# Sketched attention and squared-ReLU feed-forward on one core: another prologue, with S first, k features in column tiles, w_in in two loads and four pieces of v through GpSimd's queue

## The chip, the core and the metric

The kernel runs on one core of a Trainium2 chip. The metric is the device time of one execution in microseconds (us); lower is better. Several executions were timed, and one more was taken by the hardware profiler. All durations below come from that profiled execution.

## What is computed

Polynomial-sketch attention without a softmax, then a feed-forward block. For each of 4 batches and 4 heads (sequence 1088, head size 32):

```python
a, b = S1 @ x, S2 @ x                 # 8 values each, for x = q and x = k
phi(x) = outer(a, b)                  # 64 features per position
kv = sum_s phi(k_s) v_s^T             # 64 x 32
z  = sum_s phi(k_s)                   # 64
attn = phi(q) kv / (phi(q) z + 1e-6)
x = attn, heads side by side          # 4352 tokens x 128
out = relu(x @ w_in)**2 @ w_out       # w_in 128 x 2048, w_out 2048 x 128
```

All in float32; the product with w_in uses the rounded type fp32r, so w_in has to be converted ("cast") on the chip once.

## The kernel before, in words

The feed-forward part is TensorE's work: tokens are cut into ten chunks of columns (256, 384, 448, 448, 512 ...). For each chunk there are 16 blocks of w_in. A *unit* is one or two blocks: a first product `pg` (L589), a relu on ScalarE (`gt`, L598), a square on ScalarE or VectorE (`g`, L606 or L608), and a second product `po` (L627) that sums over the 16 blocks.

The attention part makes the columns of `xT` that these chunks read. Batches 1 to 3 are prepared while earlier chunks run. Batch 0 can't be: its first 256 columns are made in a **prologue**, written out by hand, in which nothing of the feed-forward runs. From there on a small planner in the kernel (`_Order`) places all remaining tasks on the engines, by due times and by cost estimates in its code; the engines then run in that fixed order. The rest of batch 0 (12 blocks of 32 columns from block 8, then 16 from block 20) is planned work too.

The prologue, in the order in which it feeds itself:

- Loads. SP issues k of batch 0 in two column halves, q's first 256 columns, then v, further q, w_in in four loads and w_out in four. ScalarE issues S1 and S2 (L217, L218) into `s_nat` and two pieces of v. A load that reuses one of the eight semaphores for hardware loads waits until the load eight before it has landed, so SP's list also waits in places. v of batch 0 comes as two times four pieces: first the row blocks t = 0 to 3 of four groups of partitions, then t = 4 to 8 of the same groups ("the later pieces").
- S is turned around by VectorE (`s_T`, L688), and thirteen small copies on GpSimd, VectorE and ScalarE spread it into block-diagonal tables: `sf` (for k, L693; a plain copy, L708) and `sq` (for q, L696 to L703).
- TensorE meanwhile runs ten matmuls of ones (`warm`, L678) that compute nothing.
- VectorE transposes k into `kt0` (L291) in three parts and q's first 256 columns into `qT` (L297).
- TensorE: `kf` (L314), nine fp32 products of 128 x 128 k columns with `sf`; then `x` (L729), q's sketch with `sq`, in two halves q0(0) and q0(1). ScalarE copies half of each result (`kb`, `qb`), and VectorE multiplies (`kp`, L330, four instructions; `qp`, L748).
- TensorE: `kvp` (L390), 36 products of `kp` with v, t by t; the first 16 need the first pieces of v, the rest the later ones.
- The closing chain: `bd` (L764) spreads `kvp`; the denominator `den` (L794) goes through a transpose, a reciprocal and another transpose (`dT`, `rd`, `bc`); the numerator times `bc` is `xT` (L819), which the first `pg` reads. Beside it: `zm`, the sketch with z (L801, copied to `sw` by L806), the spread of kv (`a_rep`, L433, copied by L439), and the sketch `qc` of the next 12 blocks (L304), whose two transposes of q were made by VectorE ahead of `bd`.

GpSimd converts the four quarters of w_in (L671), two in the prologue and two as planned work.

The piece of code that sets the two parts of v:

```python
def first(b, t, p):
    return NT * p + t if b else 4 * p + t if t < 4 else 16 + 5 * p + t - 4
def load_v(eng, b, p, t0=0, t1=NT):
    n = 32 * ((t1 if p < 3 else min(t1, NT - 2)) - t0)
    eng.dma_start(
        _ap(vn[b % 2], 32 * p, 32, 32 * t0, [[32 * NT, H], [1, n]]),
        bass.AP(v.tensor, v.offset + b * H * S * D + 32 * first(b, t0, p),
                [[G * D, 32], [S * D, H], [1, n]]),
    )
```

Of the kernel before, what the change touches and what calls it, by code (L numbers as in the profile page):

```python
# [104 lines left out]
def kernel(  # L105
# [20 lines left out]
    LU = 4  # L126
    W0, W3, W4 = 10, 1, 1
    ND, QT, WI, KL, QL = 2, 3.0, (1.0, 1.9), (30.0, 12.0), 4.0
# [27 lines left out]
    def sb(name, cols, dt=F32, rows=128):  # L156
        return cpool.tile([rows, cols], dt, tag=name, name=name)
# [9 lines left out]
    w_in32, w_o, w_in = sb("w_in32", 2048), sb("w_o", 2048), sb("w_in", 2048, F32R)  # L167
    s_nat, s_T = sb("s_nat", 32, rows=32), sb("s_T", 32, rows=32)

# [11 lines left out]
    def load_q(eng, b, c0, c1):  # L181
        eng.dma_start(
            qn[b % 2][:, c0:c1],
            bass.AP(q.tensor, q.offset + b * H * S * D + c0, [[G * D, 128], [1, c1 - c0]]),
        )
# [10 lines left out]
            bass.AP(  # L196
                v.tensor, v.offset + b * H * S * D + 32 * first(b, t0, p),
                [[G * D, 32], [S * D, H], [1, n]],
            ),
        )  # L200

    def load_wi(eng, c):
        eng.dma_start(
            w_in32[:, 512 * c : 512 * c + 512], moe_w_in[:, 512 * c : 512 * c + 512]
        )
# [9 lines left out]

    nc.vector.memset(s_nat[:], 0.0)
    nc.scalar.dma_start(s_nat[0:8, :], S1[:, :])  # L217
    nc.scalar.dma_start(s_nat[8:16, :], S2[:, :])  # L218
    load_k(nc.sync, 0, 0, 512)
# [8 lines left out]
    load_v(nc.scalar, 0, 3, 0, 4)  # L228
    for p in range(4):
        load_v(nc.sync, 0, p, 4, NT)  # L230
    load_q(nc.sync, 0, 256, 640)
    load_wi(nc.sync, 0)
    load_wi(nc.sync, 1)
    load_q(nc.sync, 0, 640, S)
    load_wo(nc.sync, 0)
    load_wi(nc.sync, 2)
    load_wi(nc.sync, 3)
    load_wo(nc.sync, 1)
# [5 lines left out]

    sf, sq = sb("sf", 96), sb("sq", 256)
    nc.vector.memset(sf[:, 0:64], 0.0)
    nc.gpsimd.memset(sq[:], 0.0)
    nc.gpsimd.memset(_ap(vn[0], 96, 32, 32 * (NT - 2), [[32 * NT, H], [1, 64]]), 0.0)
# [62 lines left out]
    def a_kf(t0, n, pool, tag):  # L311
        kf = pool.tile([128, 512], F32, tag=tag, name="kf")
        for t in range(n):
            nc.tensor.matmul(  # L314
                _ap(kf, 0, 128, 32 * t, [[32 * n, 2], [1, 32]]),
                kt0[:, 128 * (t0 + t) : 128 * (t0 + t) + 128],
                sf[:, 0:64],
            )
# [370 lines left out]
    for h, eng in (
        (0, nc.gpsimd.tensor_copy), (1, nc.vector.tensor_copy), (2, nc.scalar.copy),  # L690
        (3, nc.vector.tensor_copy),
    ):
        eng(  # L693
            _ap(sf, 32 * h, 32, 8 * h, [[32, 2], [1, 8]]), _ap(s_T, 0, 32, 0, [[8, 2], [1, 8]])
        )
    nc.gpsimd.tensor_copy(  # L696
        _ap(sq, 0, 32, 0, [[8, 8], [1, 8]]), _ap(s_T, 0, 32, 8, [[0, 8], [1, 8]])
    )
    nc.scalar.copy(
        _ap(sq, 0, 32, 128, [[8, 8], [1, 8]]), _ap(s_T, 0, 32, 0, [[1, 8], [0, 8]])  # L700
    )
    for h, eng in ((1, nc.scalar.copy), (2, nc.gpsimd.tensor_copy), (3, nc.scalar.copy)):
        eng(  # L703
            _ap(sq, 32 * h, 32, 64 * (h % 2), [[128, 2], [1, 64]]),
            _ap(sq, 0, 32, 0, [[128, 2], [1, 64]]),
        )
    for h in range(H):
        nc.gpsimd.tensor_copy(sf[32 * h : 32 * h + 32, 64:96], s_T[:, :])  # L708
    for h in range(H):
# [43 lines left out]
    for y in range(2):  # L753
# [27 lines left out]
    a_bd(0)  # L781

    nc.gpsimd.tensor_copy(zero_a[:, 0:1], st[0, "kp"][:, 256 * NT - 1 : 256 * NT])
    for c in range(2):
        cast_wi(c)
    nc.gpsimd.memset(sfk[:], 0.0)
    for h in range(H):
        o = 16 * (h % 2)
        nc.gpsimd.tensor_copy(sfk[32 * h : 32 * h + 32, o : o + 16], s_T[:, 0:16])
    num0 = psf.tile([128, 512], F32, tag="pg", name="num0")  # L790
# [21 lines left out]
    keep_warm(W4)
    dT0 = wpool.tile([128, 256], F32, tag="dT0", bufs=1, name="dT0")
# [30 lines left out]

    for c in (2, 3):
        O.add(("wi", c), {"POOL": 0.7}, 0.5 * c, [], on(cast_wi, c), at=WI[c - 2])
    prev = {"qc": None}
    PEL, M, T0 = 0.3, 5.0, 1.5

    def q_tasks(b, i0, nb, key):  # L850
# [3 lines left out]
        names = []  # L854
        if (b, i0) != (0, AC[0][1][0]):
            for x in range(2):
                i1, n1 = i0 + x * (nb // 2), nb // 2
                n1 = min(n1, G - i1)
                names.append(("qT", b, i1))
                O.add(  # L860
                    names[-1], {"DVE": dve(32 * n1)}, k0 - 1.5,
                    ([("qn", b)] if b else []) + prev["qTuse"], on(a_qT, b, i1, n1),
                    at=QT if i0 == 20 else 0.0,
                )
# [139 lines left out]
    for u in range(NU):  # L1004
# [90 lines left out]
```

## Time and profile before

| | |
|---|---|
| time, median of 3 runs | 187.05 us (186.77 to 187.11) |
| time of the profiled execution | 186.58 us |
| its span, first to last instruction | 184.8 us |
| TensorE matmul busy | 180.0 us, 97% |
| ScalarE, VectorE, GpSimd busy | 135.0, 120.0, 36.8 us |
| first product of the feed-forward (`pg`) | at 13.54 us |
| loads, share of the 16 DMA engines busy, 0 to 4.6 us | 0.57 (179 GB/s) |
| the same, 4.6 to 8.2 us | 0.75 (214 GB/s) |
| the same, 10.54 to 13.54 us | 0.98 (300 GB/s) |

The profile lists busy time by engine, groups of instructions by source line, the chain of work that ended last, and a timeline. "PE" is TensorE's matmul side, "PEld" its weight loads, "DVE" VectorE, "ACT" ScalarE, "POOL" GpSimd, "SP" the engine that only issues loads and stores; a "q" behind a name is that engine's instruction queue, where a load is issued. A row of the timeline gives start, duration, engine, line, what is written from what, a count if rows are merged, and in brackets how long the engine stood idle before it and what ended that.

### The profile page before, as it was taken

Reading aid. Unit: us, or ns where it says so; the run is one execution under the profiler, and the core shown is the slowest. Engines: PE = TensorE matmul, PEld = TensorE weight load, DVE = VectorE, ACT = ScalarE, POOL = GpSimd, SP = SyncE. Lnnn points to the kernel's source line nnn. Section 1 sums busy time; section 2 is a strip of 40 time slices with the busy share of each in tenths; the row PEclk is TensorE's granted clock in tenths of the full one; section 3 lists DMA queues with packets and bytes.
Section 4 is the critical chain, followed back from the end, with each engine's and each line's share of the span. In section 5 each row is a group of like instructions: output and inputs, shape, how many; then the busy total and the mean of one; then the engine's idle time right before and its main releaser. Section 6 shows DMA issues by size and latency. Waiting matters only on the chain.

```text
span 184.8 us, 3784 instructions
## 1 busy us (share of the span) xinstructions
PE 180.0 (97%) x1418; PEld 104.9 (57%) x1418; DVE 120.0 (65%) x259; ACT 135.0 (73%) x264; POOL 36.8 (20%) x162
## 2 busy tenths in 40 slices
PE   8998999999999999999999999999999999999992
PEld 2867766656555466555554545545555545555791
DVE  4979879959983598699436984998243334222430
ACT  3409869759968787699577975794777777777760
POOL 3745407138300000870000004820000000000000
PEclk9999999999999999999999999999999999999999
DMA  5799800100039700000871200003003000300211
GB/s 179 205 278 322 200 8 2 28 4 0 0 46 239 173 0 4 4 0 14 200 199 20 41 0 5 0 0 49 11 0 59 0 0 5 52 0 0 33 28 28
DMA packets 24673, 11.25 MB, mean 61 GB/s; under 512 B 18000, under 2 KB 23120, under 8 KB 24656
## 3 DMA queue, kind: packets, MB, share of 16 engines
q1 hardware_dynamic: 24144, 10.82, 24.8%
q10 hardware_dynamic: 512, 0.20, 0.4%
q8 instruction: 11, 0.18, 0.4%
q14 instruction: 6, 0.05, 0.1%
HBM read 8.78 MB, written 2.23 MB: 60 GB/s over the span
## 4 chain that ended last, share of the span: by engine, by line
PE 97%; ACT 0%; DVE 0%; issue 0%
PE po L627 60%; PE pg L589 18%; PE nd L542 4%; PE warm L678 3%; PE kvp L408 2%; PE pol L622 2%; PE po L622 2%; PE qc L304 2%; PE kvp L390 1%; PE kf L314 1%; PE kc L344 1%; PE x L729 1%; ACT gt L598 0%; PE den L794 0%; PE num L794 0%; PE den L754 0%
## 5 line engine op out<-in xcount | busy, mean ns | idle before, releaser
L627 PE MATMUL po<-g,w_o 128*128 128x512 f32 (+3 forms) x288 | 123.5, 547 | 0.0
L598 ACT ACTIVATE gt<-pg 128x512 f32<-128x512 f32 (+3 forms) x145 | 75.1, 568 | 34.6 <-PE pg L589 34.2
L627 PEld LDWEIGHTS po<-g,w_o 128*128 128x128 f32 x288 | 53.1, 188 | 31.8 <-issue 23.6
L589 PE MATMUL pg<-xT,w_in 128*128 128x512 f32 (+3 forms) x160 | 68.9, 513 | 0.5 <-ACT gt L598 0.5
L606 ACT ACTIVATE g<-gt 128x512 f32<-128x512 f32 (+2 forms) x105 | 59.9, 602 | 1.4
L608 DVE TENSOR_TENSOR g<-gt 128x512 f32<-128x512 f32 (+3 forms) x40 | 26.6, 666 | 40.6 <-ACT gt L598 40.0
L589 PEld LDWEIGHTS pg<-xT,w_in 128*128 128x128 f32 x160 | 28.9, 190 | 29.1 <-ACT gt L598 10.6
L449 POOL COPY kv<-kvt 32x64 f32<-32x64 f32 x48 | 12.3, 256 | 64.8 <-DVE kvt L426 62.7
L503 POOL COPY rd<-rc 32x9 f32<-32x9 f32 (+2 forms) x80 | 16.5, 206 | 11.2 <-DVE rc L495 7.8
L512 DVE STREAM_SHUFFLE qa<-qc 128x576 f32<-128x576 f32 (+2 forms) x20 | 11.6, 652 | 0.0
L527 DVE TENSOR_TENSOR qp<-qa,qb 128x576 f32<-128x576 f32 (+2 forms) x20 | 10.8, 606 | 0.0
L361 DVE TENSOR_TENSOR kp<-fs 128x576 f32<-128x576 f32 x12 | 8.4, 752 | 0.1
L475 DVE STREAM_TRANSPOSE qt<-qc 128x576 f32<-128x576 f32 (+2 forms) x10 | 5.8, 615 | 3.7 <-PE qc L304 3.7
L631 DVE STREAM_TRANSPOSE oT<-po 128x512 f32<-128x512 f32 (+3 forms) x9 | 5.9, 652 | 2.4 <-PE po L627 2.4
L542 PE MATMUL nd<-qp,kv 32*32 32x288 f32 (+2 forms) x320 | 6.8, 353 | 0.0
L559 DVE TENSOR_TENSOR xT<-nd,bc 128x576 fp32r<-128x576 f32 (+2 forms) x10 | 5.6, 600 | 1.2 <-PE nd L542 1.2
L552 DVE STREAM_TRANSPOSE bc<-rd 128x576 f32<-128x576 f32 (+2 forms) x10 | 5.8, 605 | 0.7 <-POOL rd L503 0.6
L542 PEld LDWEIGHTS nd<-qp,kv 32*32 32x32 f32 x320 | 3.8, 103 | 3.9 <-issue 2.9
L512 DVE STREAM_SHUFFLE qb<-qc 128x576 f32<-128x576 f32 (+2 forms) x10 | 6.0, 649 | 0.0
L297 DVE STREAM_TRANSPOSE qT<-qn 128x192 f32<-128x192 f32 (+3 forms) x11 | 5.9, 566 | 0.0
L678 PE MATMUL warm<-const-bfloat16-1.0 128*128 128x512 bf16 x12 | 5.0, 571 | 0.8 <-PEq L1079 0.8
L622 PE MATMUL pol<-w_o,g 128*128 128x128 f32 x32 | 5.7, 275 | 0.0
(96 smaller groups left out, 92.6 us busy)
## 6 DMA issues: line engine op xcount, KB each, us to landing
kn<-in_k_dram SPq DMA_DIRECT2D x3, 544.0 KB, 4.9
qn<-in_q_dram SPq DMA_DIRECT2D x3, 544.0 KB, 6.9
vn<-in_v_dram SPq DMA_DIRECT2D x9, 144.0 KB, 5.3
w_in<-in_moe_w_in_dram SPq DMA_DIRECT2D x4, 256.0 KB, 5.0
w_o<-in_moe_w_out_dram SPq DMA_DIRECT2D x4, 256.0 KB, 7.9
out_dram<-oT SPq DMA_DIRECT2D x12, 64.0 KB, 2.0
out_dram<-oT SPq DMA_DIRECT2D x8, 56.0 KB, 2.3
out_dram<-oT SPq DMA_DIRECT2D x8, 48.0 KB, 2.2
```

The lines of the kernel that those rows point to most:

```text
L449: nc.gpsimd.tensor_copy(_ap(st[b, "kv"], 32 * c, 32, 64 * h, [[32, E], [1, 32]]), _ap(st["kvt"], 32 * h, 32, 0, [[64, E], [1, 32]]),)
L503: nc.gpsimd.tensor_copy(st[b, "rd", i0][32 * h : 32 * h + 32, n * c : n * c + n], st["rc"][32 * c : 32 * c + 32, n * h : n * h + n],)
L512: nc.vector.stream_shuffle(in_=banks(st[b, "qc", i0], 2 * x, 0, m), out=_ap(st[b, which, i0], 0, 128, 2 * m * x, [[m, 2], [1, m]]), mask=m ...
L527: nc.vector.tensor_tensor(out=st[b, "qp", i0, e][:, r], in0=st[b, f"qa{e}", i0][:, r], in1=st[b, "qb", i0][:, r], op=mult,)
L542: nc.tensor.matmul(nd[32 * h : 32 * h + 32, 512 * c : 512 * c + m], kv[r, o : o + 32], qp[r, m * h : m * h + m], start=(e == 0), stop=(e = ...
L589: nc.tensor.matmul(st["pg", u][:, n * i : n * i + n], w_in[:, 128 * (d0 + i) : 128 * (d0 + i) + 128], xT[:, c0 : c0 + n],)
L598: nc.scalar.activation(gt[:, 0:w], st["pg", u][:, 0:w], Relu)
L606: nc.scalar.activation(g2[:, 0:w], gt[:, 0:w], Square)
L608: nc.vector.tensor_tensor(out=g2[:, 0:w], in0=gt[:, 0:w], in1=gt[:, 0:w], op=mult)
L622: nc.tensor.matmul(po[x // 128][:, 0:128], g[:, x : x + 128], w, start=(d == 0), stop=(d == NB - 1),)
L627: nc.tensor.matmul(po[0][:, 0:n], w, g, start=(d == 0), stop=(d == NB - 1))
L678: nc.tensor.matmul(t_[:, 0:cols], nc.const_aps.tensor(1.0, (128, 128), mybir.dt.bfloat16), nc.const_aps.tensor(1.0, (128, cols), mybir.dt. ...
```

## The change

Only the prologue is rewritten, with what follows from it in the planner's list.

- **S.** S1 is issued by ScalarE without waiting for a memset, S2 by SP as its first load. The thirteen copies go. A selection table `sel` is made on GpSimd by two copies from the identity matrix; four fp32 matmuls of `s_nat` with `sel` (K = 16, 32 x 80 each) make all tables for k and the plain S in PSUM; ScalarE copies them once into `ss`. `s2f` is then transposed at once by VectorE, ahead of k's transposes. `sq` is made by two products on GpSimd (128 x 128 each, two inputs).
- **Dummy matmuls:** five, then the four of S, then three; later one rather than two.
- **k features:** each of the nine 128-column products is cut into four of 32 columns, whose outputs lie in four groups of 32 partitions.
- **Loads:** w_in comes in two loads of 1024 columns rather than four of 512, the first one ahead of q's second part; one w_out load moves ahead of q's third part. The four later pieces of v leave SP and are issued by GpSimd, after the two copies into `sel` and ahead of `sq`.
- **Casts of w_in:** two quarters on ScalarE behind `qb`, two on GpSimd behind its small work; none is planned work any more.
- **The end of the prologue:** the copy of `kvt` goes from VectorE to ScalarE; the numerator is placed ahead of the spread of kv; the two transposes for `qc` and `qc` itself leave the prologue and become planned work.

The core of the diff:

```diff
-    W0, W3, W4 = 10, 1, 1
+    W0, W1, W3 = 5, 3, 1
...
-    nc.vector.memset(s_nat[:], 0.0)
     nc.scalar.dma_start(s_nat[0:8, :], S1[:, :])
-    nc.scalar.dma_start(s_nat[8:16, :], S2[:, :])
+    nc.sync.dma_start(s_nat[8:16, :], S2[:, :])
     load_k(nc.sync, 0, 0, 512)
     load_k(nc.sync, 0, 512, S)
     load_q(nc.sync, 0, 0, 256)
...
-    for p in range(4):
-        load_v(nc.sync, 0, p, 4, NT)
+    load_wi(nc.sync, 0)
     load_q(nc.sync, 0, 256, 640)
-    load_wi(nc.sync, 0)
     load_wi(nc.sync, 1)
+    load_wo(nc.sync, 0)
     load_q(nc.sync, 0, 640, S)
-    load_wo(nc.sync, 0)
-    load_wi(nc.sync, 2)
-    load_wi(nc.sync, 3)
...
-    nc.gpsimd.memset(sq[:], 0.0)
+    sq, sel = sb("sq", 256), sb("sel", 320, rows=16)
+    nc.vector.memset(sel[:, :], 0.0)
...
+    nc.gpsimd.tensor_copy(
+        _ap(sel, 0, 16, 0, [[88, 4], [32, 2], [1, 8]]), _ap(iden, 0, 16, 0, [[0, 4], [8, 2], [1, 8]])
+    )
+    nc.gpsimd.tensor_copy(
+        _ap(sel, 0, 16, 64, [[80, 4], [1, 16]]), _ap(iden, 0, 16, 0, [[0, 4], [1, 16]])
+    )
+    for p in range(4):
+        load_v(nc.gpsimd, 0, p, 4, NT)
...
-            nc.tensor.matmul(
-                _ap(kf, 0, 128, 32 * t, [[32 * n, 2], [1, 32]]),
-                kt0[:, 128 * (t0 + t) : 128 * (t0 + t) + 128],
-                sf[:, 0:64],
-            )
+            for c in range(4):
+                o = 128 * (t0 + t) + 32 * c
+                nc.tensor.matmul(
+                    _ap(kf, 32 * c, 32, 32 * t, [[32 * n, 2], [1, 32]]),
+                    kt0[:, o : o + 32],
+                    sf,
+                )
...
-        nc.gpsimd.tensor_copy(
+        (nc.scalar.copy if c < 2 else nc.gpsimd.tensor_copy)(
             w_in[:, 512 * c : 512 * c + 512], w_in32[:, 512 * c : 512 * c + 512]
         )
...
+    sp = psf.tile([128, 512], F32, tag="po", name="sp")
+    for h in range(H):
+        nc.tensor.matmul(
+            sp[32 * h : 32 * h + 32, 0:80], s_nat[:, :], sel[:, 80 * h : 80 * h + 80]
+        )
+    nc.scalar.copy(ss[:, :], sp[:, 0:80])
+    nc.vector.transpose(s2f[:, :], _ap(ss, 0, 128, 72, [[0, 4], [1, 8]]))
+    keep_warm(W1)
     a_kT0(0, 4)
-    nc.vector.transpose(s_T[:, :], s_nat[:, :])
...
+    for x in range(2):
+        nc.gpsimd.tensor_tensor(
+            out=_ap(sq, 0, 128, 128 * x, [[64, 2], [8, 8], [1, 8]]),
+            in0=_ap(ss, 0, 128, 72 - 8 * x, [[0, 2]] + [[[0, 8], [1, 8]], [[1, 8], [0, 8]]][x]),
+            in1=_ap(own_q, 0, 128, 0, [[1, 2], [0, 8], [0, 8]]),
+            op=mult,
+        )
...
-    for i0 in (8, 14):
-        a_qT(0, i0, 6)
...
+    for c in range(4):
+        cast_wi(c)
     a_bd(1)
...
+    nc.scalar.copy(st["kvt"][:, :], st[0, "kvp"][:, 0:128])
...
+    nc.scalar.copy(sw[0][:, 16:24], x0[:, 384:392])
+    nd0(num0, 0)
     a_rep(x0, 256)
-    nc.scalar.copy(sw[0][:, 16:24], x0[:, 384:392])
     a_rep_kv(x0, 256)
-    nd0(num0, 0)
     st["warm"] = psf.tile([128, 512], F32, tag="po", name="warm")
     keep_warm(W3)
-    a_qc(0, *AC[0][1])
-    keep_warm(W4)
```

More of the change, by code (lines that the diff above doesn't have):

```diff
@@ L167 @@
     w_in32, w_o, w_in = sb("w_in32", 2048), sb("w_o", 2048), sb("w_in", 2048, F32R)
-    s_nat, s_T = sb("s_nat", 32, rows=32), sb("s_T", 32, rows=32)
+    s_nat, ss, s2f = sb("s_nat", 32, rows=16), sb("ss", 80), sb("s2f", 32)
+    sf, s_T = ss[:, 0:64], ss[:, 64:80]
     sw = [sb(f"sw{i}", 32) for i in range(2)]
@@ L203, in load_wi @@
         eng.dma_start(
-            w_in32[:, 512 * c : 512 * c + 512], moe_w_in[:, 512 * c : 512 * c + 512]
+            w_in32[:, 1024 * c : 1024 * c + 1024], moe_w_in[:, 1024 * c : 1024 * c + 1024]
         )
@@ L240 @@
     load_wo(nc.sync, 3)
-    sf, sq = sb("sf", 96), sb("sq", 256)
-    nc.vector.memset(sf[:, 0:64], 0.0)
-    nc.gpsimd.memset(sq[:], 0.0)
+    sq, sel = sb("sq", 256), sb("sel", 320, rows=16)
+    nc.vector.memset(sel[:, :], 0.0)
     nc.gpsimd.memset(_ap(vn[0], 96, 32, 32 * (NT - 2), [[32 * NT, H], [1, 64]]), 0.0)
@@ L262 @@
     make_identity(nc, iden[:])
-    own_f, s2f, zm = sb("own_f", 16), sb("s2f", 32), sb("zm", 32)
+    own_f, zm = sb("own_f", 16), sb("zm", 32)
+    own_h, own_q = sb("own_h", 4), sb("own_q", 2)
+    nc.gpsimd.tensor_copy(
[6 more added lines that the diff above has]
+        load_v(nc.gpsimd, 0, p, 4, NT)
+    nc.vector.tensor_reduce(
+        out=own_h[:, :], in_=_ap(iden, 0, 128, 0, [[32, 4], [1, 32]]), op=add, axis=AX
+    )
+    nc.vector.tensor_tensor(out=own_q[:, :], in0=own_h[:, 0:2], in1=own_h[:, 2:4], op=add)
     nc.vector.tensor_reduce(
@@ L267 @@
     )
-    nc.vector.memset(kT[:, S:SP], 0.0)
-    nc.vector.memset(qT[:, S:SP], 0.0)
     mask_a = [[4 * e + l // 8 for l in range(32)] for e in range(E)]
@@ L463, in a_w @@
             in0=_ap(st[b, "kvp"], 0, 128, 32, [[64, E], [8, 4], [1, 8]]),
-            in1=_ap(sf, 0, 128, 72, [[0, E], [0, 4], [1, 8]]),
+            in1=_ap(ss, 0, 128, 72, [[0, E], [0, 4], [1, 8]]),
             op=mult,
@@ L686 @@
     keep_warm(W0)
-    a_kT0(0, 4)
-    nc.vector.transpose(s_T[:, :], s_nat[:, :])
[L689 to L694, printed above, removed]
-        )
[L696 to L708, printed above, removed]
+    sp = psf.tile([128, 512], F32, tag="po", name="sp")
[6 more added lines that the diff above has]
+    keep_warm(W1)
+    a_kT0(0, 4)
+    for x in range(2):
[4 more added lines that the diff above has]
+            op=mult,
+        )
     for h in range(H):
@@ L715 @@
     for w in sw:
-        nc.gpsimd.tensor_copy(w[:, :], sf[:, 64:96])
+        nc.gpsimd.memset(w[:, 16:32], 0.0)
+        nc.gpsimd.tensor_copy(w[:, 0:16], s_T)
+    nc.gpsimd.tensor_tensor(
+        out=_ap(sfk, 0, 128, 0, [[16, 2], [1, 16]]),
+        in0=_ap(ss, 0, 128, 64, [[0, 2], [1, 16]]),
+        in1=_ap(own_q, 0, 128, 0, [[1, 2], [0, 16]]),
+        op=mult,
+    )
+    nc.gpsimd.memset(kT[:, S:SP], 0.0)
+    nc.gpsimd.memset(qT[:, S:SP], 0.0)
     nc.gpsimd.memset(_ap(pd, 0, 128, 8, [[9, 4 * NT], [1, 1]]), 1e-6)
@@ L745 @@
             a_kv0(t)
-    nc.vector.transpose(s2f[:, :], _ap(sf, 0, 128, 72, [[0, 4], [1, 8]]))
     nc.vector.tensor_tensor(
@@ L769, in a_bd @@
         )
+    for c in range(4):
+        cast_wi(c)
     a_bd(1)
-    st["kvt"] = wpool.tile([128, 128], F32, tag="kvt", name="kvt")
-    nc.vector.tensor_copy(st["kvt"][:, :], st[0, "kvp"][:, 0:128])
     nc.vector.tensor_tensor(
@@ L781 @@
     a_bd(0)
[L783 to L789, printed above, removed]
+    st["kvt"] = wpool.tile([128, 128], F32, tag="kvt", name="kvt")
+    nc.scalar.copy(st["kvt"][:, :], st[0, "kvp"][:, 0:128])
     num0 = psf.tile([128, 512], F32, tag="pg", name="num0")
@@ L843, in on @@
         return lambda eng: f(*args)
-    for c in (2, 3):
-        O.add(("wi", c), {"POOL": 0.7}, 0.5 * c, [], on(cast_wi, c), at=WI[c - 2])
     prev = {"qc": None}
@@ L854, in q_tasks @@
         names = []
[L855 to L864, printed above, removed]
+        for x in range(2):
+            i1, n1 = i0 + x * (nb // 2), nb // 2
+            n1 = min(n1, G - i1)
+            names.append(("qT", b, i1))
             O.add(
-                ("qc", b, i0), {"PE": 0.75}, k0 - 1.0, names + [("w", b)], on(a_qc, b, i0, nb),
-                rings=[("att", 1)], lag=PEL,
-            )
-        else:
-            O.add(("qc", b, i0), {"PE": 0.01}, -99.0, [], lambda eng: None, rings=[("att", 1)])
+                names[-1], {"DVE": dve(32 * n1)}, k0 - 1.5,
+                ([("qn", b)] if b else []) + prev["qTuse"], on(a_qT, b, i1, n1),
+                at=QT if i0 == 20 else 0.0,
+            )
+        O.add(
+            ("qc", b, i0), {"PE": 0.75}, k0 - 1.0, names + [("w", b)], on(a_qc, b, i0, nb),
+            rings=[("att", 1)], lag=PEL,
+        )
         prev["qTuse"] = [("qc", b, i0)] if i0 + nb == 4 * NT else []
@@ L888, in q_tasks @@
                 ("rl", b, i0, c), {"POOL": 0.8}, k0 + 0.1 * c, [], on(a_rl, b, i0, nb, c),
-                uses=[("rc", b, i0)] + [("wi", 3)], rings=[("rd", 2)] if c == 0 else [],
+                uses=[("rc", b, i0)], rings=[("rd", 2)] if c == 0 else [],
             )
@@ L1016 @@
                 mm1s[i], {"PE": n / 2400 + 0.01},
-                tu[u] - LA + 0.001 * i, xt + [("wi", (d0 + i) // 4)] * (u < NB), on(ffn1, u, i),
+                tu[u] - LA + 0.001 * i, xt, on(ffn1, u, i),
                 rings=[("pg" if u else "po", 2)] if i == 0 else [], lag=0.05,
```

## The prediction

> **What bounds the kernel now.** I read the chain of waits first, by line, then the timeline of the first 25 us, where alone the change acts.
>
> ```profile
> PE 180.0 (97%) x1418; PEld 104.9 (57%) x1418; DVE 120.0 (65%) x259; ACT 135.0 (73%) x264; POOL 36.8 (20%) x162
> ...
> PE 97%; ACT 0%; DVE 0%; issue 0%
> ```
>
> The chain is TensorE almost throughout, so behind the first `pg` only TensorE work counts, and the change leaves that work as it is: in the built programs the later order is the same but for a few swaps. What can move is the start of the first `pg`, 13.54. It hangs on the prologue, some of whose matmuls are dummies. The timeline's rows of 0 to 24 us (start, duration, engine, line, tiles):
>
> ```profile
> 1.80 0.29 POOL masks.py:199 TENSOR_SCALAR_AFFINE_SELECT iden<-iden 128x128 f32<-128x128 f32 x1
> ...
> 3.37 0.71 DVE L291 STREAM_TRANSPOSE kt<-kn 128x512 f32<-128x512 f32 x1 [0.82 <-DMA kn<-in_k_dram]
> ...
> 4.95 2.08 PEld L314 LDWEIGHTS kf<-sf,kt 128*128 128x128 f32 x18 [0.66 <-POOL sq L696]
> ...
> 4.98 2.19 PE L314 MATMUL kf<-sf,kt 128*128 128x64 f32 x18
> ...
> 5.63 0.40 DVE L297 STREAM_TRANSPOSE qT<-qn 128x256 f32<-128x256 f32 x1
> ...
> 5.96 2.71 DVE L330 TENSOR_TENSOR kp<-kf,kb 128x512 f32<-128x512 f32 x4
> ...
> 7.11 1.14 PE L729 MATMUL x<-qT,sq 64*128 64x256 f32 x8
> ...
> 8.17 2.32 PE L390 MATMUL kvp<-vn,kp 128*64 128x64 f32 x72
> ...
> 10.54 0.29 DVE L764 TENSOR_TENSOR bd<-kvp,own_p 128x128 f32<-128x128 f32 x1 [0.39 <-PE kvp L390]
> ```
>
> Read it backwards. `bd` at 10.54 waits for `kvp`, and from `bd` to the first `pg` is a fixed 3.00 us (den, dT, rd, bc, xT). `kvp` runs without a gap from 8.17, 2.37 before `bd`. Its first factor was ready at about 6.6 (5.96 plus the first of four products), so it waited only for TensorE: `x` came first (1.06 from 7.11 to 8.17), and `x` stood behind `kf`, which ended at 7.17. So the prologue is bound by TensorE from 4.98, by VectorE's `kp` just behind (ended 8.67), and by loads ahead of that.
>
> **Part by part.**
>
> *S and `kf`.* Gone: thirteen copies, whose last one released `kf` at 4.95. New: four S matmuls, a ScalarE copy, `s2f`. S is issued at about 0.73 instead of 0.92 and 1.52; k's two loads and q's first one move back by one issue, 0.3 to 0.4 (S1's issue took 0.58, S2's 0.29). Five dummies at 0.42 end at 2.9, S matmuls about 3.3, the copy of 80 columns (rows of `kb`: 0.21) 3.6, `s2f` (0.19) 3.8. k's first half lands at 3.7 (was 0.73 + 2.6 = 3.35), its transpose (0.71) ends at 4.5. So `kf` may begin 0.45 earlier. Column tiles replace 18 weight loads at 0.116 (2.08/18) by 72 of a quarter of the columns. The nearest row, `kvp`'s half-width tiles, takes 2.32/72 = 0.032 each, 2.3 in all, no gain; if four run beside each other as `kvp`'s two do, half of it, 1.1. I take 1.1; at 2.3 `kf` would end near 7.1 as now.
>
> *VectorE's order* then sets the pace. k's second half landed at 1.19 + 3.0 = 4.2 and q at 1.66 + 3.7 = 5.4. Now they come 0.35 later at issue, and ScalarE's two pieces of v (64 KB each, at 1.90 and 3.37 so far) go out ahead of 2 us beside them: 128 KB at 300 GB/s is 0.4. I take k at 5.0 and q at 5.5 to 5.8, from no change to 0.8 later. Two transposes (0.84) and `qT` (0.40) end at 6.25, `kp` begins 6.2 rather than 5.96. After `qT`, `x` may start at 6.4, and 1.06 + 2.37 later `bd` at **9.85**: 0.69 earlier. That is the floor if nothing else is late.
>
> *GpSimd's queue* is what can be late. Four loads are put between the copies into `sel` and the products `sq`, and all of `x`, hence `kvp`, stands behind `sq` on TensorE. From 1.10 (the memset of v's padding) to the end of the identity at 2.09 are 0.99; without the memset of `sq` ahead they start at 0.73, so 1.72, and two copies (0.19 to 0.23 each) make 2.15. An issue costs I. Two products of 128 columns: the nearest one-input rows are 0.29; with two inputs I take 0.40 each (0.3 to 0.6), 0.8. `sq` is done at 2.95 + 4I. TensorE starts the second half of `x` 0.16 later (as `den` behind `bd`), it takes 0.53, then 2.37: `bd` at **6.01 + 4I**. What else stands behind the four issues has time: `irep` (1.32 for four copies), a memset (0.31) and `sw` (0.35) end near 9.4, and are read by the spread of kv and by `qc`, at 11.5 and later. SP in turn has four v issues and two of w_in fewer, so q's later parts, w_out and batch 1 go out earlier; none of them was waited for by TensorE, so I count nothing.
>
> No load was issued by GpSimd in this trace, so I is bounded by the rows of v's pieces on the other queues:
>
> ```profile
> L194 SPq DMA_DIRECT2D vn<-in_v_dram x10: 311/431/1802, 2.1 to 16.1; - x10
> L194 ACTq DMA_DIRECT2D vn<-in_v_dram x2: 343/360/378, 1.9 to 3.4; - x2
> ```
>
> The columns are shortest, median and longest issue in ns. Below is 0.31, the shortest (four cost 1.2, the floor holds); above 1.80, the longest, in which SP was held up. No row is nearer to an issue whose descriptors a processor writes, so I take the middle, 1.05: `bd` at 10.21, 0.33 earlier. Each 0.1 of I is 0.4 us; the prologue breaks even at 1.13.
>
> On this the Trainium skill speaks against the change: "DMA: Bandwidth & Descriptors", section "Latency and other measured facts", puts the first byte of a load of GpSimd's queue at about 1 us, made by its cores, against about 0.6 for the hardware queues. By an estimate that takes this 1 us for I, `bd` would be at 10.01, 0.53 earlier; no run here shows it yet.
>
> *The later pieces of v.* `kvp` needs them 16/36 of the way in, at I = 1.05 about 7.84 + 1.03 = 8.9, and the last one is issued at 6.35. Pieces of 80 KB landed 2.5 after issue, those of 64 KB 3.5: 0 to 0.9 late. I take 0, as SP, no longer holding them, has its first w_in load out early and the engines were only 0.57 and 0.75 busy to 8.2.
>
> *Casts.* Two on ScalarE (GpSimd's took 0.61 each) between `qb` and `kvt`: ScalarE stood idle for 3.58 there, so they hide if w_in lands by 9.3; a w_in load landed 5.0 after issue and this one, twice as long, is issued near 3.5. If it is 1 us late, `kvt` is, and only the spread of kv, which `xT` doesn't read.
>
> *`qc` as planned work* (0.45 on TensorE, two transposes of 0.63 on VectorE) was beside the division chain, so its removal saves nothing. It now lies behind the first four `pg`, where TensorE waits for relu:
>
> ```profile
> 14.82 0.47 PE L589 MATMUL pg<-xT,w_in 128*128 128x256 f32 x2 [0.48 <-ACT gt L598]
> ...
> 18.94 0.75 PEld L542 LDWEIGHTS nd<-qp,kv 32*32 32x32 f32 x64 [0.23 <-issue]
> ```
>
> The transposes end 0.5 after the first `pg`, `qc` fits the gap: 0. If not, up to 0.45. The 12 blocks' sketch starts 1.4 later on VectorE, but GpSimd's casts no longer hold `rd` (they ended at 16.72, `rc` was there at 15.85); `nd` is moved behind two more `po`, so its wait of 0.23 goes. I take 0.2 gained, from 0.3 lost to 0.4 gained.
>
> **Sum**: 0.33 + 0.2 = 0.53 off the profiled execution's 186.58, that is 186.05. The median of the runs lies 0.47 above it, so I predict 187.05 - 0.53 = **186.5**.
>
> **Rivals.**
>
> 1. *GpSimd becomes the bound* (the slower side): four issues ahead of `sq`. From I = 1.18 the gain of 0.2 is used up too, and at 1.4 `bd` is at 11.61: 187.05 + 1.07 - 0.2 = 187.9. At 1.80 it is 189.5. For it: every product of TensorE's prologue behind `kf` waits for one queue. Against it: GpSimd has 2 us of nothing to do from 2.1 to 4.45 now.
> 2. *Issues are cheap* (below 0.96): the floor, 9.85, and 187.05 - 0.69 - 0.2 = 186.2; with q no later than now 185.9.
> 3. *v comes late*: the four pieces share the engines with w_in, 512 KB at a time. At 3.5 to landing `kvp` stands still for 0.9 to 1.0: 187.05 + 0.6 - 0.2 = 187.4.
> 4. *TensorE's clock*: with only eight dummies and a hole at 2.9, full clock could come later. The profile's clock row is 9 from the first slice, yet the first ten dummies took about 0.6 each, and one at 12.78 took 0.39. A half-speed `x` and half of `kvp` cost 1.06 + 1.2 less what VectorE hides, about 1.5: 188.3.
>
> **How the numbers follow.** Chances: the forecast (I from 0.97 to 1.15) 0.34, of which 0.10 is too small to measure; rival 2 0.25; rival 1 0.25, of which 0.05 within; rival 3 0.10, half of it within; rival 4 0.06. A measurement of this kernel tells about 0.2%, 0.37 us, from no change. Faster by more: 0.24 + 0.25 = 0.49. Within: 0.10 + 0.05 + 0.05 = 0.20. Slower: 0.20 + 0.05 + 0.06 = 0.31. The range takes in rival 2's 185.9 and rivals 1 and 3 to 188.2, leaving out dear issues above 1.45. The forecast's own range is 186.1 to 187.0.
>
> **What would show it.** Right: `bd` between 9.8 and 10.3, first `pg` 3.0 behind it, `x` released by `sq` on GpSimd, four issues of about 1 us in POOL's queue. Rival 2: `x` released by `qT`. Rival 1: `sq` after 7.7. Rival 3: `kvp` with a hole that a landing of v ends. Rival 4: dummies or `x` at doubled spacing after 5 us. I am wrong on the ramp if the work from the first `pg` to the first 384-column `pg` (13.54 to 21.86) takes longer than 8.3.

## The result, and the profile after

The changed kernel takes 187.85 us (median of 7 runs, 187.38 to 188.17) against 187.08 for the kernel before on the same chip: ratio 1.0038, 95% interval 1.0025 to 1.0050. It is 0.7 to 0.8 us slower, not 0.5 faster. The profiled execution took 187.43 (before 186.58), its span is 185.5 (184.8). Medians and ratios here and below leave out executions in a slower state: one of before's seven here, and nine of twelve in e17, whose median with them is 191.53.

The page, by engine and then the chain that ended last, by engine and by line:

```profile
PE 179.3 (97%) x1476; PEld 104.2 (56%) x1477; DVE 119.5 (64%) x254; ACT 135.9 (73%) x264; POOL 36.4 (20%) x159
...
PE 92%; DMA 3%; POOL 1%; issue 1%; DVE 0%; POOLq 0%
PE po L635 60%; PE pg L597 18%; PE nd L550 3%; DMA vn<-in_v_dram 3%; PE kvp L416 2%; PE pol L630 2%; PE po L630 2%; PE qc L310 2%; PE kc L352 1%; PE kvp L398 1%; POOL vn L195 1%; PE num L794 0%; PE den L794 0%; PE den L764 0%; PE x L441 0%
```

A load stands in the chain: a piece of v, 3% of the span, with its issue on GpSimd (`POOL vn L195`) ahead of it. Before, the chain was TensorE's alone. The timeline's rows, for the steps shown of before:

```profile
1.45 0.29 POOL masks.py:199 TENSOR_SCALAR_AFFINE_SELECT iden<-iden 128x128 f32<-128x128 f32 x1
...
2.17 2.36 POOL L195 DMA_DIRECT2D vn<-in_v_dram  x4
...
4.06 0.71 DVE L297 STREAM_TRANSPOSE kt<-kn 128x512 f32<-128x512 f32 x1
4.54 0.77 POOL L705 TENSOR_TENSOR sq<-ss,own_q 128x128 f32<-128x128 f32 x2
...
4.92 1.86 PE L322 MATMUL kf<-ss,kt 128*32 128x64 f32 x72
...
5.93 0.43 DVE L303 STREAM_TRANSPOSE qT<-qn 128x256 f32<-128x256 f32 x1
6.28 2.71 DVE L338 TENSOR_TENSOR kp<-kf,kb 128x512 f32<-128x512 f32 x4
...
6.71 1.13 PE L740 MATMUL x<-qT,sq 64*128 64x256 f32 x8
...
7.78 1.15 PE L398 MATMUL kvp<-vn,kp 128*64 128x64 f32 x32
...
10.13 1.39 PE L398 MATMUL kvp<-vn,kp 128*64 128x64 f32 x40 [1.20 <-DMA vn<-in_v_dram]
...
11.55 0.29 DVE L771 TENSOR_TENSOR bd<-kvp,own_p 128x128 f32<-128x128 f32 x1 [1.96 <-PE kvp L398]
...
14.47 0.74 PE L597 MATMUL pg<-xT,w_in 128*128 128x256 f32 x4 [0.61 <-DVE xT L817]
15.14 0.23 PEld L310 LDWEIGHTS qc<-qT,sw 32*32 32x32 f32 x32
...
20.81 0.75 PEld L550 LDWEIGHTS nd<-qp,kv 32*32 32x32 f32 x64 [0.33 <-DVE bc L560]
```

Read it down. Four issues on GpSimd take 0.59 each, `sq` is done at 5.31, `x` begins at 6.71 (before 7.11) and `kvp` at 7.78 (8.17): up to here the change gains 0.4. Then `kvp`, one group of 72 records before, falls into 32 and 40 with 1.20 between them, ended by v. `bd` is 1.01 later than before, the first `pg` 0.93.

The table of transfers (engine that issued, count, size, median us from the begin of the issue to landing) shows GpSimd's three pieces of 80 KB, two of v's first pieces, which SP issues in the same stretch (2.51 and 2.99), and GpSimd's last piece of 48 KB; the second fence is the last piece in the kernel before.

```profile
vn<-in_v_dram POOLq DMA_DIRECT2D x3, 80.0 KB, 4.4
...
vn<-in_v_dram SPq DMA_DIRECT2D x2, 64.0 KB, 4.6
...
vn<-in_v_dram POOLq DMA_DIRECT2D x1, 48.0 KB, 6.0
```

```profile
vn<-in_v_dram SPq DMA_DIRECT2D x1, 48.0 KB, 1.8
```

Issued at 3.98, the last piece lands at 9.99; before, issued at 5.4, it landed at 7.2. SP's pieces were no quicker (4.6) than GpSimd's first ones (4.4).

### The profile page after: what moved, and what is told of

Read it like the earlier page. It is cut to its first block, busy times and chain, and to the rows that moved or that the text cites. A ratio compares the mean times of both kernels' runs of the same rounds, so it can differ in the third digit from the quotient of the medians.

```text
span 185.5 us, 3891 instructions
## 1 busy us (share of the span) xinstructions
PE 179.3 (97%) x1476; PEld 104.2 (56%) x1477; DVE 119.5 (64%) x254; ACT 135.9 (73%) x264; POOL 36.4 (20%) x159
## 4 chain that ended last, share of the span: by engine, by line
PE 92%; DMA 3%; POOL 1%; issue 1%; DVE 0%; POOLq 0%
PE po L635 60%; PE pg L597 18%; PE nd L550 3%; DMA vn<-in_v_dram 3%; PE kvp L416 2%; PE pol L630 2%; PE po L630 2%; PE qc L310 2%; PE kc L352 1%; PE kvp L398 1%; POOL vn L195 1%; PE num L794 0%; PE den L794 0%; PE den L764 0%; PE x L441 0%
## 5 line engine op out<-in xcount | busy, mean ns | idle before, releaser
L630 PE MATMUL po<-w_o,g 128*128 128x128 f32 x32 | 5.7, 275 | 0.0
```

Of the source, the lines that this page charges most:

```text
L630: nc.tensor.matmul(po[x // 128][:, 0:128], g[:, x : x + 128], w, start=(d == 0), stop=(d == NB - 1),)
```

## The experiments

Seventeen kernels. The table gives the median, the ratio to the kernel before on the same chip with its 95% interval, and from the profiled execution: when full clock was granted (the trace's clock record; the page's clock row is 9 throughout because that record has no entry ahead of the first grant), the start of `x`, the hole in `kvp` (TensorE's idle time between its two halves), `bd` and the first `pg`. "Held" means that w_in is issued only after GpSimd's `sq`; "dummies" are matmuls that compute nothing; SyncE in the expectations is SP.

| kernel | median | ratio [95%] | clock | x | hole | bd | pg |
|---|---|---|---|---|---|---|---|
| before | 187.1 | 1 | 4.63 | 7.11 | 0 | 10.54 | 13.54 |
| changed | 187.85 | 1.0038 [1.0025, 1.0050] | 6.21 | 6.71 | 1.20 | 11.55 | 14.47 |
| e1 v on SP | 186.74 | 0.9997 [0.9980, 1.0014] | 9.02 | 7.38 | 0 | 11.60 | 14.52 |
| e2 w_in held | 186.46 | 0.9979 [0.9960, 0.9999] | 6.46 | 7.08 | 0 | 10.53 | 13.45 |
| e4 only v on GpSimd | 187.35 | 1.0016 [1.0007, 1.0026] | 5.73 | 7.62 | 0 | 11.18 | 14.19 |
| e5 v behind w_in | 187.52 | 1.0021 [1.0011, 1.0031] | 6.96 | 7.19 | 0.38 | 11.20 | 14.13 |
| e3 w_in in four | 186.98 | 1.0003 [0.9987, 1.0018] | 9.68 | 7.34 | 0 | 11.85 | 14.76 |
| e6 more dummies | 187.48 | 1.0028 [1.0014, 1.0043] | 5.72 | 7.17 | 0.60 | 11.43 | 14.35 |
| e7 held, dummies | 186.34 | 0.9964 [0.9951, 0.9977] | 4.60 | 7.11 | 0 | 10.55 | 13.47 |
| e8 SP, dummies | 186.75 | 0.9991 [0.9977, 1.0005] | 6.82 | 7.18 | 0 | 10.61 | 13.53 |
| e9 kf whole | 186.76 | 0.9987 [0.9973, 1.0000] | 4.03 | 7.32 | 0 | 10.75 | 13.67 |
| e11 four, S2 on ScalarE | 187.92 | 1.0049 [1.0032, 1.0066] | 7.23 | 7.63 | 0 | 11.06 | 13.98 |
| e12 SP, S2 on ScalarE | 187.80 | 1.0057 [1.0035, 1.0079] | 8.70 | 7.98 | 0 | 11.74 | 14.66 |
| e13 held, S2 on ScalarE | 188.22 | 1.0061 [1.0043, 1.0079] | 8.92 | 8.18 | 0 | 11.96 | 14.87 |
| e14 SP, short dummies | 186.65 | 0.9981 [0.9962, 0.9999] | 6.27 | 6.88 | 0 | 10.31 | 13.23 |
| e15 held, short dummies | 186.01 | 0.9951 [0.9938, 0.9963] | 5.12 | 7.13 | 0 | 10.56 | 13.48 |
| e16 four, short dummies | 186.87 | 0.9994 [0.9982, 1.0006] | 5.20 | 6.87 | 0.71 | 11.24 | 14.17 |
| e10 late part alone | 187.88 | 1.0041 [1.0027, 1.0055] | 6.33 | 7.88 | 0 | 11.31 | 14.22 |
| e17 w_in on GpSimd | 187.77 | 1.0078 [1.0036, 1.0121] | 4.61 | 7.04 | 2.52 | 14.22 | 18.28 |

My theory: v's later pieces are late because they share the DMA engines with w_in. Rivals: GpSimd's queue is slow by itself; the order against w_in is to blame whichever queue carries v; the loss is elsewhere in the prologue (S, the clock).

### Which part makes v late: e1, e2, e5, e4

e1, on the changed kernel:

```diff
+    for p in range(4):
+        load_v(nc.sync, 0, p, 4, NT)
     load_wi(nc.sync, 0)
...
-    for p in range(4):
-        load_v(nc.gpsimd, 0, p, 4, NT)
```

> The changed kernel, with the four later pieces of v issued by SyncE ahead of w_in, as before the change. Main theory (the pieces come late because GpSimd's queue gets its turn on the DMA engines only beside w_in): they land by 7.5, kvp runs without its hole of 1.20, bd falls from 11.55 to 10.15 to 10.35, the first pg from 14.47 to 13.1 to 13.3, and the time is 1.2 to 1.4 below the changed kernel's: ratio to the kernel before 0.996 to 0.998. Rival (the loss is in the rest of the prologue: full clock from 6.2 instead of 4.6, S on the matrix path, SyncE's first slot): bd stays at 10.9 or later and the ratio at 1.000 or above. If w_in, issued four issues later, is now late, a wait for it shows ahead of the first pg and half the gain is gone.

The hole is gone, `bd` is not earlier. The profiled execution met something else:

```profile
7.38 1.92 PE L740 MATMUL x<-qT,sq 64*128 64x256 f32 x8
...
9.23 2.32 PE L398 MATMUL kvp<-vn,kp 128*64 128x64 f32 x72
```

`x` takes 1.92 instead of 1.13, since full clock came only at 9.02. Of the twelve times seven lie from 186.29 to 186.78 and five from 187.41 to 187.92; the profiled one (187.47) is of the upper five. So both theories hold in part: v was late, and a second loss stood behind it in this execution. When the others got full clock isn't on record.

e2, on the changed kernel; SP's loads from w_in on (w_in, q's further parts, w_out) stand behind the memset in the program:

```diff
+    nc.gpsimd.memset(w_in32[:, 0:1], 0.0)
     load_wi(nc.sync, 0)
     load_q(nc.sync, 0, 256, 640)
```

> The changed kernel, v still through GpSimd's queue, but a one-column memset of w_in's raw tile by GpSimd behind sq (5.3) makes SyncE hold w_in and all that it issues behind it until then; the memset's column is overwritten by the load. Main theory (contention with w_in): the later pieces land by 7.6 and the hole of 1.20 shrinks to 0.1 or less, bd near 10.2, time 1.0 to 1.4 below the changed kernel's if w_in (landing near 10.5 and 12.5) is still in time. Rival (the latency of GpSimd's own queue): the pieces land at 9.3 and 10.0 again, the hole stays at 1.0 to 1.2 and the time within 0.3 of the changed kernel's.

The same queue, the same issues at 2.17; only w_in and what follows it come later. `kvp` is one group again, and the last piece takes 4.0:

```profile
8.16 2.32 PE L390 MATMUL kvp<-vn,kp 128*64 128x64 f32 x72
```

```profile
vn<-in_v_dram SPq DMA_DIRECT2D x2, 64.0 KB, 4.9
...
vn<-in_v_dram POOLq DMA_DIRECT2D x1, 48.0 KB, 4.0
```

That decides for contention. Issued at the same time on the same queue, the last piece lands at 7.94 instead of 9.99, ahead of the 8.93 at which `kvp` would have needed it in the changed kernel: 2.0 of the 6.0, and all of the lateness, come from w_in and the loads behind it. It repeats: 4.0 in e7, e9 and e15 too, 5.9 in e6, where w_in is not held. The 4.0 itself, 2.2 more than before, is not shown to be GpSimd's queue: before's piece was issued 1.4 later, and SP's own piece, issued at 2.50 in e2, took 4.9. The median is 1.4 below the changed kernel's, as this theory had it, though the twelve times spread over 2.1.

e5, on e1: the four lines stand behind `load_wi(nc.sync, 0)` instead of ahead of it.

> The changed kernel, with the later pieces of v issued by SyncE directly behind the first w_in load (512 KB). If the order against w_in alone is to blame, whichever queue carries v, the pieces land at 9.3 to 10.0 as in the changed kernel and the hole is 0.9 to 1.2. Main theory: on one queue they follow w_in's 512 KB directly, land between 8.3 and 8.9, hole 0 to 0.3, time 0.9 to 1.3 below the changed kernel's.

```profile
9.78 1.39 PE L398 MATMUL kvp<-vn,kp 128*64 128x64 f32 x40 [0.38 <-DMA vn<-in_v_dram]
```

On one queue, behind 512 KB, the last piece (issued at 6.2, 3.4 to landing) lands at 9.65, not far from the 9.99 on GpSimd's queue beside it, though issued 2.2 later. In e1, where SP has v ahead of w_in, it landed at 7.99. So w_in's first load ahead of v costs 1.7 on SP's own queue, 0.4 of it by the later issue: the order against w_in makes v late, more than the queue. The hole is near the theory's; the time is not (0.33 below the changed kernel's, by the medians), because `x` began 0.48 later than there.

e4, on the kernel before: the four issues of v go to GpSimd behind `make_identity`, nothing else.

> The kernel before, with this one part alone: the four later pieces of v issued by GpSimd behind the identity, SyncE's four issues gone. Main theory: w_in moves up by four issues, the pieces land between 8 and 9.6, and kvp, whose second half began near 9.2, stands still for 0.1 to 0.8; sf and sq on GpSimd, behind the issues, add 0 to 0.4 at kf: 0.3 to 1.0 slower than before. Latency of the queue alone: pieces at 9.3 and 10.0, 0.8 to 1.2 slower. Rival of the rest of the prologue: no hole, within 0.4 of before.

Slower by 0.16%, and for neither reason: no hole (the last piece took 5.0, and `kvp` began 0.65 later than before). `kf` began at 5.29 because S landed at 4.4 to 4.5 (before by 4.2); GpSimd's issues were over by 4.57 and did not hold it.

### Smaller rows of w_in, and the clock: e3, e6, e7, e8

e3, on the changed kernel: w_in in loads of 512 columns, two, q's second part, two.

> The changed kernel, with w_in in four loads of 512 columns (rows of 2048 instead of 4096 bytes) in the same place of SyncE's order: two, q's second part, two. If GpSimd's packets take turns with w_in's one by one, halving w_in's rows lets v through sooner: last piece at 9.2 to 9.7 instead of 9.99, hole 0.5 to 0.9 instead of 1.20, time 0.3 to 0.7 below the changed kernel's. If only the bytes in flight count, landings, hole and time stay within 0.2 of the changed kernel's.

The last piece took 5.1 and there is no hole, but the clock (9.68) made `x` so late that none could show. Inconclusive; e16 repeats it.

e6 on the changed kernel, e7 on e2 and e8 on e1 add two dummies:

```diff
-    W0, W1, W3 = 5, 3, 1
+    W0, W1, W3 = 5, 4, 1
...
     keep_warm(W0)
+    keep_warm(1, 160)
```

> The changed kernel, with a short dummy (160 columns) ahead of the S matmuls and a fourth one behind them, so that TensorE has no hole from 0.8 to 5.1; kf begins at 5.1 instead of 4.9. If late v sets the end of kvp, whatever the clock, kvp's second half still begins at 10.1 and the time is within 0.3 of the changed kernel's. If the later full clock (6.2 there, 4.6 before) is what costs, the first pg comes 0.5 to 1.0 earlier.

> The run with w_in held back to 5.3, with the same two dummies added. Its twelve times fell in two groups, 185.8 to 186.6 and 187.3 to 187.9. If the upper group comes from executions in which a hole in TensorE's work at 2.9 and 4.7 put off full clock, it goes away: all times within 0.8 of each other, median 186.1 to 186.5, x always at 1.13. If the groups have another cause, they stay (a quarter of the times above 187.2).

> The run with the later pieces of v back on SyncE, with the same two dummies added. Its profiled execution had x at 1.92 instead of 1.13 and full clock only at 9.0; its times fell in two groups, 186.3 to 186.8 and 187.4 to 187.9. If the hole of 0.45 ahead of kf and the one at 2.9 put off full clock, x takes 1.13, the first pg comes at 13.2 to 13.5 instead of 14.5, the upper group goes away and the median is 186.2 to 186.6. If not, 186.7 with two groups again.

e6: `x` begins 0.46 later and `kvp`'s second half still at 10.01, so late v sets the end there, and the clock does not; the intervals of its ratio and the changed kernel's overlap.

```profile
10.01 1.39 PE L398 MATMUL kvp<-vn,kp 128*64 128x64 f32 x40 [0.60 <-DMA vn<-in_v_dram]
```

e7: all five times within 0.31 (e2: 2.1), as expected of filled holes; but with three of e2's twelve above 187.2, five low ones in a row would come about one time in four by chance (an estimate, 0.75 to the fifth power). e8: `x` at 1.13 and `pg` at 13.53, but the times still spread from 186.30 to 187.76; dummies alone did not make one group of them.

### What holds the cured kernels: e9, e11, e12, e13

e9, on e7: the tiles of `kf` undone.

```diff
-            for c in range(4):
-                o = 128 * (t0 + t) + 32 * c
-                nc.tensor.matmul(
-                    _ap(kf, 32 * c, 32, 32 * t, [[32 * n, 2], [1, 32]]),
...
+            nc.tensor.matmul(
+                _ap(kf, 0, 128, 32 * t, [[32 * n, 2], [1, 32]]),
...
```

> The run with w_in held back and two more dummies, with kf's column tiles undone (eighteen products of 128 columns at 0.112, 2.1 in all, instead of 1.43 without the waits). If the tiles are off the path that sets the end (x waits for qT at 6.97 there, and x began at 7.11), x begins at 7.2 to 7.3 and the time is 0 to 0.2 longer. If they carry the gain, x begins at 7.5 or later and the time is 0.4 to 0.8 longer.

`x` is 0.21 later, the first `pg` 0.20, the median 0.4. The tiles are worth 0.2 in the trace; the other 0.2 of the medians I can't place, and the intervals allow it.

e11 (e3), e12 (e1) and e13 (e2) fill TensorE with short dummies and put S2 back on ScalarE:

```diff
-    nc.sync.dma_start(s_nat[8:16, :], S2[:, :])
+    nc.scalar.dma_start(s_nat[8:16, :], S2[:, :])
...
     keep_warm(W0)
+    keep_warm(1, 160)
...
     keep_warm(W1)
+    keep_warm(1, 224)
```

> The changed kernel with w_in in four loads, S2's load back on ScalarE's queue and short dummies (160 columns ahead of the S matmuls, 224 behind the three) that fill TensorE to 5.0. SyncE then issues k and q one place earlier: k at 3.7, q at 5.6, qT at 5.9, x at 6.6 to 6.9, kvp without a hole, bd at 10.0 to 10.3, median 185.9 to 186.4. Rival: v through GpSimd's queue is still late, kvp stands 0.3 or more and the median is 186.6 or above.

> The run with the later pieces of v back on SyncE, with S2's load back on ScalarE's queue and the same short dummies to 5.0. x at 6.6 to 6.9, no hole, bd at 10.0 to 10.3, median 186.0 to 186.4 and one group of times. If w_in, issued near 6, is late, ScalarE's cast ends behind 12 and holds kvt: the first pg is then later than bd by more than 3.0.

> The run with w_in held back to 5.3, with S2's load back on ScalarE's queue and the same short dummies to 5.0. q at 6.1 instead of 6.47, x at 6.7 to 6.9 instead of 7.1, bd at 10.1 to 10.3, median 185.9 to 186.3. If GpSimd's pieces of v, in flight beside q, are what makes q late, q stays at 6.4 and the median at 186.3 to 186.5.

All three medians lie 1.4 to 1.9 above the expected ranges. The row of the S matmuls in e13:

```profile
4.11 0.49 PE L690 MATMUL sp<-sel,s_nat 16*32 16x80 f32 x8 [0.91 <-DMA s_nat<-in_S_dram]
```

With S2 on SP they began at 3.13. As ScalarE's second load S2 is issued at 1.35 instead of 0.74 and the S matmuls wait for it until 3.86 to 4.11; the dummies and `kf` queue behind them (5.86 to 6.10), TensorE has a hole of 0.66 to 0.91 and full clock comes at 7.2 to 8.9. S2's place at the head of SP, which I had priced only by the 0.3 it takes from k, is what makes the early S early.

### The best order: e14, e15, e16, e17, and the late part: e10

e14, e15 and e16 are e1, e2 and e3 with the short dummies and S2 on SP.

> The run with the later pieces of v back on SyncE (S2 on SyncE as in the change), with short dummies (160 columns ahead of the S matmuls, 224 behind the three) to 5.0. If the four full dummies were what held kf at 5.36 there, kf begins at 5.0 to 5.15, x at 6.8 to 7.1, bd at 10.2 to 10.5, the first pg at 13.1 to 13.4, median 186.2 to 186.6 in one group. If full clock still comes late in some executions, the times spread over 1 us or more and the median stays at 186.7.

> The run with w_in held back to 5.3, with the short dummies instead of full ones. q, landing near 6.4 beside GpSimd's packets, then sets x (7.0 to 7.1), so nothing is gained over the full dummies: bd at 10.4 to 10.55, median 186.2 to 186.5. If the full dummies held it, x at 6.8 and the median at 186.0 to 186.2.

> The changed kernel with w_in in four loads, S2 on SyncE as in the change, and the short dummies. If smaller rows of w_in are a cure and its first run was only held up by the clock (full at 9.7 there, x at 2.08), the last piece lands at 9.0 to 9.3, the hole is 0 to 0.3, bd at 10.2 to 10.6 and the median at 186.3 to 186.7. If v is still the limit, hole 0.5 or more and the median at 187.0 or above.

e14 has the earliest `bd` (10.31), and the ramp gives 0.3 back: w_in's second load, issued at 7.22, lands at 13.75, GpSimd casts it from 13.80, and the twentieth `pg` behind the first comes after 14.50 instead of 14.19. Its times lie from 186.15 to 188.24. e15 beats both kernels, 0.5% below before, all five times from 185.97 to 186.44, though its profile shows `x` no earlier than before: VectorE waits for k's second half, which lands at 5.69 (5.42 in e7, with the same loads), and `kf` and `x` follow it.

```profile
5.71 0.84 DVE L289 STREAM_TRANSPOSE kt<-kn 128x384 f32<-128x384 f32 x2 [0.90 <-DMA kn<-in_k_dram]
...
7.13 1.13 PE L743 MATMUL x<-qT,sq 64*128 64x256 f32 x8
...
10.56 0.29 DVE L774 TENSOR_TENSOR bd<-kvp,own_p 128x128 f32<-128x128 f32 x1 [0.45 <-PE kvp L390]
```

e16 missed: with rows half as large the hole is still 0.71, the last piece takes 5.7, and `kvp`'s second half begins 0.31 earlier than in the changed kernel. The line of that half is

```profile
9.82 1.39 PE L400 MATMUL kvp<-vn,kp 128*64 128x64 f32 x40 [0.71 <-DMA vn<-in_v_dram]
```

Smaller rows are no cure; the median, 186.87, lies between the two expectations.

e17, on e14: the exchange of the queues.

```diff
-    load_wi(nc.sync, 0)
...
-    load_wi(nc.sync, 1)
...
+    for c in range(2):
+        load_wi(nc.gpsimd, c)
```

> The two queues' loads exchanged, with short dummies as before: the later pieces of v on SyncE behind the first ones, w_in's two loads through GpSimd's queue behind sq (issued near 4.8 and 5.4). If GpSimd's packets in flight beside k and q are what kept x at 7.1 in the run with w_in held back, x begins at 6.8 to 6.95, kvp has no hole and bd is at 10.2 to 10.35; w_in then lands by 11, the way from the first pg to the end is 171.1 to 171.2, and the median is 185.7 to 186.1. If w_in through GpSimd's queue is later than 11.5, or v on SyncE is late beside it, the median is 186.3 or above.

Now w_in is GpSimd's and v is SP's, and v is later still. One row of the timeline, one of the table of transfers and one of the windows (stretch, sum, busy time of PE, PEld, DVE, ACT and POOL, granted clock, DMA share, GB/s):

```profile
11.78 2.40 PE L396 MATMUL kvp<-vn,kp 128*64 128x64 f32 x40 [2.52 <-DMA vn<-in_v_dram]
```

```profile
vn<-in_v_dram SPq DMA_DIRECT2D x1, 48.0 KB, 5.7
```

```profile
12.00:16.00 4.00, 4.00 (x48) 2.58 (x46) 0.59 (x3) 0.27 (x1) 0.61 (x2) 0.50 1.10 359
```

With the hole of 2.52 the clock went back to half, from 11.44 to 21.68, and the first `pg` came at 18.28. The profiled execution took 192.25; its half clock goes with the kernel's own hole, and the twelve times reach from 187.59 to 192.84. The expectation's question is answered as well: `x` began at 7.04 and k's second half landed at 5.59, although GpSimd's first packet moved only at 6.14. So GpSimd's packets are not shown to be what kept `x` at 7.1 in e15; that stays open.

e10, on the kernel before: from the end of `kvp` on as in the changed kernel, and w_in in two loads in the places of the first and third of four.

```diff
-    for i0 in (8, 14):
-        a_qT(0, i0, 6)
...
+    for c in range(4):
+        cast_wi(c)
     a_bd(1)
...
-    a_qc(0, *AC[0][1])
-    keep_warm(W4)
```

> The kernel before with the late part of the change alone (qc as planned work, its transposes with it, two of the four casts and kvt on ScalarE, num ahead of the spread of kv, w_in in two loads in the places of the first and the third of four); the prologue up to bd and v's queue as before. The prediction gave this part 0.2, from 0.3 lost to 0.4 gained: first pg at 13.4 to 13.7, from there to the end 0.1 to 0.3 less than 171.3, ratio 0.998 to 1.000. If w_in's first load, landing near 10.7, makes kvt late, the first pg comes later than 13.7 and the ratio is above 1.000.

From the first `pg` to ScalarE's last output copy it takes 166.85 (before 166.87): nothing gained and nothing lost. The prologue, which it leaves alone up to `bd`, was 0.77 later: S's transpose began 0.25 later, full clock came at 6.33, `kf` took 2.71 instead of 2.19. All five times are above before's median; when the other four got full clock isn't on record, and why all five lie high stays open. The late part need not cost that: e7 and e15 have all of it and are faster than before.

## Why the prediction was wrong

- **The bound**: right. Only the first `pg` moved; `bd` to `pg` is 2.92 (predicted 3.00), and ScalarE's last output copy moved by 0.84 with the first `pg`'s 0.93.
- **S and `kf`**: missed, without deciding the end. `kf` began at 4.92, not 4.5 (before: 4.98): k's transpose began at 4.06, not near 3.8, and the three dummies behind the S matmuls, which the sum leaves out, ran to 4.9. Tiles: 1.43 at full clock without the waits (e7), between the 1.1 taken and the 2.3; worth 0.2 (e9).
- **VectorE's order**: right, `kp` 6.28 (6.2).
- **GpSimd's queue**: the mechanism was not the bound. I is 0.59, not 1.05, and lies below 0.96, where rival 2 began. By the formula `sq` is done at 5.31, as measured. `x` ran right behind `kf`; rival 1 did not happen.
- **"The later pieces of *v* ... I take 0"**: this is the step that failed. I carried before's times from issue to landing (2.5 for 80 KB, 3.5 for 64 KB) over to the new order and bounded the lateness by 0.9, and I read room on the DMA engines from before's busy shares (0.57 and 0.75), although the change itself puts 512 KB there. Measured: 4.0 without w_in beside it (e2, e15), 6.0 with it. The last issue began at 3.98; my sum has it from 5.30 to 6.35 and counts the landing from its end, while the 2.5 and 3.5 are counted from the begin. v was thus issued 1.3 earlier than I assumed, and `kvp`'s second half still began 1.20 behind its time, 8.93. Rival 3 had the mechanism, with a chance of 0.10. That it had the hole to 0.3 was partly luck: it has v land near 9.85 (6.35 plus 3.5), measured is 9.99 (3.98 plus 6.0), so two errors nearly cancel. Its 187.4 is 0.45 low.
- **Without the hole** `kvp` of that execution would end at 10.10 and `bd` stand near 10.15 (predicted 10.21); that sum is argued. The variants of the changed kernel without a hole and with full clock by 7 reached 10.31 (e14) to 10.75 (e9, without the tiles): in them `kf` or q came later than in the changed kernel.
- **Ramp**: mis-sized. First `pg` to ScalarE's last output copy takes 166.78 against 166.87: 0.09 of the 0.2; `qc` hid in the gap, as costed, but the wait ahead of `nd` stayed (0.33).
- **Clock** (rival 4): it did not decide the changed kernel (e6), where the wait for v hides it. In e1's profiled execution it did; that it makes the two groups of e1's times, about 0.9 apart, is likely and not shown. Before's profiled execution, with its grant at 4.63, lies 0.50 below its median and the changed kernel's 0.42 below its own, so these two traces can be compared; e1's lies 0.73 above its median.

The Trainium skill, "DMA: Bandwidth & Descriptors", section "Queues, rings and completion order", says that each DMA engine takes turns between its queues, one packet of several descriptors at a time. The turns fit what is seen: v waits beside w_in whichever of the two sits in GpSimd's queue (1.20 in the changed kernel, 2.52 in e17). No run here shows a turn itself. The figure that the prediction cites from the same page puts GpSimd's first byte 0.4 behind that of the hardware queues. It is a latency, and not the 0.59 for which an issue occupies GpSimd, in whose place the prediction's estimate tried it. The traces have a difference of that kind: the first packet moved 0.9 after the first issue began on SP's queue (1.67 after 0.74 in the changed kernel, on idle engines) and 1.4 to 2.3 after it on GpSimd's, beside other loads. It is not what made v late: GpSimd's and SP's pieces issued side by side took 4.4 and 4.6 to land, and w_in beside the last one added 2.0.

## What to carry to other kernels

A load moved to another queue keeps its bytes and loses its place in the order: price it by when it lands, with everything the same change puts on the engines beside it, and not by the issuing engine's time. Where a small load is needed soon and a large one late, hold the large one back (e15: 0.5% faster than before, where the change as made was 0.4% slower). Compare profiled executions of a short prologue only after looking at when each got full clock.

## What the runs showed of the hardware

- **Issue on GpSimd**: 0.55 to 0.72 us for each of the four loads of v, against 0.31 to 0.45 for most on SP and ScalarE; the first packet of GpSimd's queue moved 2.3 after the first issue began in the changed kernel, 1.9 in e4 and 1.4 in e17 (w_in, issued at 4.70).
- **The time to landing goes by what else is in flight more than by the queue**: in the changed kernel v's pieces issued from 2.2 to 3.0 took 4.6 on SP's queue (64 KB) and 4.2 to 4.4 on GpSimd's (80 KB); for v's last piece w_in ahead of it turned 2.2 into 3.4 on SP's queue (e1, e5), and w_in beside it 4.0 into 6.0 on GpSimd's (e2, the changed kernel).
- **Full clock comes in steps.** In the profiled executions it lasts 180.906 or 177.493 us, one step of 3.413 apart, and e17's was 6.827, then half for 10.240: two and three steps. The grant fell between 4.03 and 6.82 where TensorE had work from 0.8 to about 5, between 6.21 and 9.68 in the runs with the change's own dummies (holes at 2.9 and 4.7), and between 7.23 and 8.92 with a hole of 0.66 to 0.91. The Trainium skill, "TensorE: Matmul & The Clock Gate", part "What's actually happening", gives a free-running window of 3413 ns; the steps of 3.413 agree.
- **The clock can be lost again early**: e17's 2.52 us without matmuls (9.26 to 11.78) go with half clock from 11.44 on, for 10.24 us; the changed kernel's 1.20 (8.93 to 10.13) cost no clock.
